# Attention followed by routed experts: routing transposed in small squares on VectorE, single units' rows made stationary, first biases computed apart

## The chip, the cores and the metric

The kernel runs on one core of one Trainium2 chip. The metric is device time in microseconds (us). The kernel before takes 783.4 us; where two kernels are compared, each was run several times on the same chip in alternation. The engines are TensorE (PE in the profile, its weight loads PEld), VectorE (DVE), ScalarE (ACT), GpSimd (POOL) and SyncE (SP).

## The reference

Selective attention over 8 batches x 8 heads x 576 positions x 64, then a mixture of 8 experts in which each token either chooses its own expert or keeps the one of the token before it:

```python
scores = scale * q @ k.T                       # causal
bias = -(cum[:, :, :, None] - cum[:, :, None, :])   # cum = cumsum(max(s, 0))
attn = softmax(where(causal, -1e9, scores + minimum(bias, 0)))
x = (attn @ v) -> (B, S, H * D)                # D of the experts = 512
for b in range(B):
    prev_e = -1
    for s in range(S):
        fresh_e = argmax(logits[b, s])         # logits = x @ w_gate, 8 experts
        e = fresh_e if s == 0 or local_gate[b, s] < 0.5 else prev_e
        prev_e = e
        h = maximum(x[b, s] @ w1[e], 0)        # 512 -> 1024
        out[b, s] = softmax(logits[b, s])[e] * (h @ w2[e])
```

## The kernel before

TensorE works through 32 pairs of heads, one after the other. Beside them the routing of finished batches runs in groups (batches 0 and 1, 2 and 3, 4, 5), its steps planned into certain pairs. The chosen expert of a token lies with tokens on the partitions; to carry it forward along the sequence ("held") it has to lie along the free axis, so it is transposed, scanned, and transposed back. Before, TensorE did both transposes, by matmuls with the identity into a bank of the score pool (banks are parts of PSUM, the memory that TensorE writes):

```python
for bs in ((0, 1), (2, 3), (4,), (5,)):
    n = HP * bs[-1] + HP + 1
    g = sort.group(bs, xs)
    at(n, 2, g.choose, g.codes)
    at(n + 1, 1, g.rows)
    at(n + 1, 2, g.fresh, g.share, g.held)
    at(n + 2, 1, g.hold)
    at(n + 2, 2, g.hot, g.gates)
    at(n + 3, 1, g.count)
    at(n + 3, 2, g.rank)
    for f in g.scatters:
        place = max(place + (2 if n < 17 else 1), 3 * (n + 4))
        at(place // 3, (3, 4, 0)[place % 3], f)
# ... (cut)
def rows(self, bank):                     # class Group
    self.codes_of = main, tails = [x[:nb] for x in bank(2)]
    for t, p, z, a in s.runs:
        # ... (cut)
        nc.tensor.transpose(y, x, i)
def fresh(self, bank):
    for x, a in zip(self.codes_of, (0, TS)):
        # ... (cut)
        nc.vector.tensor_scalar(u[:, a:z], x, 0.0, None, Alu.is_equal)
        nc.scalar.activation(v[:, a:z], x, Act.Relu, bias=self.s.minus[: self.nb])
def hold(self, bank):
    e = self.e = bank(1)[0][:, : NB * nb].rearrange("p (t b) -> p t b", b=nb)
    for t, p, z, a in s.runs:
        # ... (cut)
        nc.tensor.transpose(e[:z, t], x, i)
```

After attention come the experts in units of rows: doubles (256 rows of one expert), singles (128 rows) and mixed units (two experts of 64 rows each). The first layer of a double or a single keeps the weights stationary and moves the rows; a mixed unit keeps the rows stationary and moves the weights, 512 columns at a time, and VectorE then turns its hidden rows:

```python
def layer1(i, first, last):
    # ... (cut)
    if len(w) > 1:                        # mixed
        # ... (cut)
                for h in range(2):
                    d = slice(h * HALF, h * HALF + HALF)
                    mm(ps[d], lhsT=xT[i][:, c, d], rhs=w[h][:, c, f], start=(c == 0), stop=(c == DK - 1))
            nc.scalar.activation(hx[i][:, f], ps, Act.Relu)
        # then 16 nc.vector.transpose of hx into hT
        return
    # double or single: matmuls of n = 256 or 128 columns
                mm(y, lhsT=w[0][:, c, f : f + P], rhs=xT[i][:, c, :], start=(c == 0), stop=(c == DK - 1))
```

At the start, 18 matmuls with the identity (`spin(18)`) warm TensorE up, all biases of the exponentials are made in one block, and only then do the first scores begin.

## Time and profile before

| kernel before | value | where it is read |
|---|---|---|
| time | 783.39 us (782.95 to 784.17) | runs |
| span of the profiled execution | 782.4 us | head of the page |
| attention, first to last rows of a pair | 17.93 to 233.28, so 215.35 us | chain of waits |
| the experts' first matmul | 241.87 us | timeline |

TensorE is busy all the time, so the table to watch is where its pairs and units start. In the chain of waits the line "PE o L406 x99" comes once in each pair: the attention-weighted rows. The lines themselves stand in the prediction. Of the 576 positions the last 64 (576 = 4 x 128 + 64) are called the tail.

### The profile page before, as it was taken

The numbers are of one execution on the slowest core, as the hardware profiler recorded it, in microseconds if no ns is written. First come the engines' busy times: TensorE is split into PE (matmuls) and PEld (weight loads), VectorE is DVE, ScalarE is ACT, GpSimd is POOL, SyncE is SP. The second block draws the span as 40 slices with busy tenths as digits, with TensorE's granted clock in tenths as the row PEclk, the third lists the DMA queues.
The fourth block names the chain that finished last, engine by engine and source line by source line (L and its number), as shares of the span: only waits on it lengthen the run. The fifth ranks groups of instructions, "written<-read, shape, count | busy, mean of one in ns | idle before, by whom it ended". The sixth has DMA issues, their size and how long they took to land.

```text
span 782.4 us, 17629 instructions
## 1 busy us (share of the span) xinstructions
PE 773.0 (99%) x6782; PEld 546.2 (70%) x6782; DVE 339.0 (43%) x1196; ACT 237.2 (30%) x611; POOL 176.2 (23%) x329
## 2 busy tenths in 40 slices
PE   9999999999999999999999999999999999999996
PEld 8888888888887846836677366773657736676762
DVE  2334444455566748315562156521565215635000
ACT  5777767776762111111111111111111111111110
POOL 4432345456450421011110111101111011011001
PEclk9999999999999999999999999999999999999999
DMA  9586679988655499966997569976699766994001
GB/s 314 187 300 194 201 244 327 326 285 262 210 208 217 131 354 390 409 228 221 376 395 297 199 224 380 392 290 208 233 365 389 297 211 228 368 409 175 10 13 44
DMA packets 64141, 205.56 MB, mean 263 GB/s; under 512 B 8269, under 2 KB 8301, under 8 KB 64048
## 3 DMA queue, kind: packets, MB, share of 16 engines
q1 hardware_dynamic: 55008, 173.55, 62.3%
q0 software_dynamic: 8896, 30.47, 10.4%
q8 instruction: 55, 0.90, 0.5%
q10 hardware_dynamic: 144, 0.33, 0.1%
q14 instruction: 38, 0.31, 0.1%
HBM read 181.08 MB, written 23.76 MB: 262 GB/s over the span
## 4 chain that ended last, share of the span: by engine, by line
issue 58%; PE 32%; POOL 5%; DVE 2%; POOLq 2%; DMA 1%; DVEq 0%
PE o L406 14%; PE ps L335 11%; POOL out_dram L1261 2%; POOL xg L1196 2%; PE hp L1243 2%; PE o L374 2%; PE o L291 1%; POOLq L1171 1%; DMA x_rows<-x,r_slot_i 1%; PE o L356 1%; PE bank L956 0%; DVE xT L1097 0%; POOL x_rows L1047 0%; PE bank L1107 0%; PE bank L981 0%
## 5 line engine op out<-in xcount | busy, mean ns | idle before, releaser
L1097 DVE STREAM_TRANSPOSE xT<-xg 32x128 f32<-32x128 f32 x576 | 174.1, 302 | 174.2 <-PE hp L1243 92.7
L1256 PE MATMUL yp<-w,hT 128*128 128x512 f32 (+1 forms) x528 | 216.4, 593 | 0.0
L1243 PE MATMUL hp<-xT,w 128*128 128x256 f32 (+1 forms) x1088 | 192.3, 337 | 0.3 <-DVE xT L1097 0.3
L1243 PEld LDWEIGHTS hp<-xT,w 128*128 128x128 f32 x1088 | 172.1, 191 | 24.6 <-issue 8.2
L344 ACT ACTIVATE sc<-ps,bias 128x256 f32<-128x256 f32 (+3 forms) x448 | 156.5, 482 | 53.6 <-PE ps L335 51.2
L1256 PEld LDWEIGHTS yp<-w,hT 128*128 128x128 f32 (+1 forms) x528 | 90.1, 180 | 114.6 <-issue 113.3
L1261 POOL DMA_INDIRECT out_dram<-y,at_gate x38 | 38.5, 1013 | 433.9 <-ACT y L1260 419.0
L406 PE MATMUL o<-v,sc 128*64 128x74 f32 x3072 | 113.6, 228 | 0.8 <-issue 0.8
L406 PEld LDWEIGHTS o<-v,sc 128*64 128x64 f32 x3072 | 108.8, 136 | 8.1 <-issue 4.3
L1247 ACT ACTIVATE hT<-hp 128x512 f32<-128x512 f32 x68 | 40.6, 597 | 193.0 <-PE hp L1243 193.0
L1260 ACT ACTIVATE y<-yp,at_gate 128x512 f32<-128x512 f32 x38 | 26.1, 687 | 239.8 <-PE yp L1256 233.6
L335 PE MATMUL ps<-q,k 64*128 64x320 f32 (+2 forms) x768 | 92.5, 386 | 0.1
L350 POOL TENSOR_SCALAR_AFFINE_SELECT sc<-sc 128x256 f32<-128x256 f32 x160 | 66.5, 420 | 115.9 <-issue 59.1
L335 PEld LDWEIGHTS ps<-q,k 64*128 64x128 f32 x768 | 68.9, 186 | 20.0 <-issue 4.8
L1256 PE MATMUL yp<-x,hT 128*128 128x512 f32 (+1 forms) x144 | 63.2, 594 | 0.0
L1234 DVE STREAM_TRANSPOSE hT<-x 32x256 f32<-32x256 f32 x64 | 27.9, 436 | 65.4 <-ACT x L1228 64.5
L1243 PEld LDWEIGHTS hp<-xT,x 128*128 128x128 f32 x320 | 46.1, 191 | 5.8 <-issue 2.6
L1243 PE MATMUL hp<-xT,x 128*128 128x128 f32 (+1 forms) x320 | 50.1, 317 | 0.0
L416 DVE RECIPROCAL recs<-o 128x4 f32<-128x4 f32 x64 | 12.1, 189 | 87.0 <-PE o L406 63.1
L1256 PEld LDWEIGHTS yp<-x,hT 128*128 128x128 f32 (+1 forms) x144 | 25.3, 178 | 26.2 <-issue 26.0
L1047 POOL DMA_INDIRECT x_rows<-x,r_slot_i x40 | 38.7, 968 | 10.1 <-issue 5.9
L419 DVE TENSOR_TENSOR x<-o,recs 128x292 f32<-128x292 f32 x64 | 34.4, 538 | 2.2
(162 smaller groups left out, 339.8 us busy)
## 6 DMA issues: line engine op xcount, KB each, us to landing
w<-in_w_dram SPq DMA_DIRECT2D x184, 512.0 KB, 9.5
x<-in_w_dram SPq DMA_DIRECT2D x56, 512.0 KB, 9.3
v<-in_vx_dram SPq DMA_DIRECT2D x32, 405.0 KB, 5.8
vt<-in_vz_dram SPq DMA_DIRECT2D x32, 320.0 KB, 3.9
k<-in_kz_dram SPq DMA_DIRECT2D x31, 320.0 KB, 5.1
q<-in_q_dram SPq DMA_DIRECT2D x32, 288.0 KB, 5.4
xg<-x_rows POOLq DMA_DIRECT2D x30, 293.0 KB, 8.5
x_rows<-r_empty SPq DMA_DIRECT2D x6, 293.0 KB, 3.6
```

The lines of the kernel that those rows point to most:

```text
L335: mm(ps[:, h, at : at + z - a], lhsT=kb[d, c * P : c * P + P], rhs=qb[d, a:z], start=True, stop=True)
L344: nc.scalar.activation(scs[n, u][:, h, at : at + z - a], raw[u][:, h, at : at + z - a], Act.Exp, bias=bias[:, i : i + 1], scale=scale)
L350: nc.gpsimd.affine_select(out=x, in_=x, compare_op=Alu.is_ge, fill=0.0, base=0, pattern=[[0, 2], [1, P]], channel_multiplier=-1)
L406: mm(y, lhsT=w, rhs=x, start=start, stop=stop)
L419: nc.vector.tensor_tensor(x, y, rec.unsqueeze(3).to_broadcast([P, t1 - t0, 2, HW]), op=Alu.mult)
L1047: self.s.nc.gpsimd.indirect_dma_start(out=next(self.s.views)[:, :], out_offset=bass.IndirectOffsetOnAxis(ap=self.slot[:z, m : m + 1], axis=0),
L1097: self.nc.vector.transpose(self.xT[i][d : d + m, :, k * P + a * m : k * P + a * m + m], rows[a * m : a * m + m, :, X0[d // DH] + d % DH :] ...
L1234: nc.vector.transpose(hT[i][d : d + m, :, a : a + m], x[a : a + m, :, d : d + m])
L1243: mm(y, lhsT=w[0][:, c, f : f + P], rhs=xT[i][:, c, :], start=(c == 0), stop=(c == DK - 1))
L1247: nc.scalar.activation(hT[i][:, g : g + per], ps, Act.Relu)
L1256: mm(ps[n * m : n * m + m, :], lhsT=hT[i][:, c, a : a + m], rhs=wn[:, c, :], start=(c == 0), stop=(c == FK - 1))
L1261: nc.gpsimd.indirect_dma_start(out=next(outs)[:, :], out_offset=bass.IndirectOffsetOnAxis(ap=at[i, k][:, 0:1], axis=0), in_=y[:, :], eleme ...
```

## The change

Its intent: take the fourteen small matmuls of each routing group from TensorE and let VectorE transpose 32x32 squares instead, which needs no bank; give the single units the form that the mixed ones have, so that eight matmuls of 512 columns replace 32 of 128; and start the first scores before all biases are there. Steps of the routing after the codes move one pair later. The diff also holds small edits that are not shown: the order of work in the last pair, the last group's scatters spread over more places, and at the experts the order of one fetch and one buffer less for the results. Cut to its core:

```diff
-            at(n + 1, 1, g.rows)
-            at(n + 1, 2, g.fresh, g.share, g.held)
-            at(n + 2, 1, g.hold)
-            at(n + 2, 2, g.hot, g.gates)
-            at(n + 3, 1, g.count)
-            at(n + 3, 2, g.rank)
+            at(n + 1, 2, g.rows, g.fresh, g.share)
+            at(n + 2, 2, g.held, g.hold)
+            at(n + 3, 2, g.hot, g.gates)
+            at(n + 4, 1, g.count)
+            at(n + 4, 2, g.rank)
             for f in g.scatters:
-                place = max(place + (2 if n < 17 else 1), 3 * (n + 4))
+                place = max(place + (2 if n < 17 else 1), 3 * (n + 5))
@@ start (cut)
-    spin(18)
+    spin(8)
+    tail_scores(0)
+    scores(0, 0)
+    # biases of group 0, their copy, scores(0, 1), then biases of group 1
@@ rows
+        if self.by_squares:
+            self.erow = self.t("row", [SQ, 3, 256])
+            for p, t, i, r in self.squares():
+                nc.vector.transpose(self.erow[:, i, r], self.code_squares[p, t, :])
+            return
@@ fresh
+        if self.by_squares:
+            # ... (cut)
+            nc.vector.tensor_scalar(u, v, 0.0, None, Alu.is_equal)
+            nc.scalar.activation(v, v, Act.Relu, bias=self.s.minus[:SQ])
+            return
@@ hold
+        if self.by_squares:
+            for p, t, i, r in self.squares():
+                nc.vector.transpose(e[p, t, :], self.erow_parts[:, i, r])
+            return
@@ layer1
-        if len(w) > 1:
+        if nbs[i] == 1:
+            m = P // len(w)
-                    for h in range(2):
-                        d = slice(h * HALF, h * HALF + HALF)
-                        mm(ps[d], lhsT=xT[i][:, c, d], rhs=w[h][:, c, f], ...)
+                    for h, wh in enumerate(w):
+                        d = slice(h * m, h * m + m)
+                        mm(ps[d], lhsT=xT[i][:, c, d], rhs=wh[:, c, f], ...)
```

## The prediction

> **What bounds the kernel now.** First the page's head: which engine is full, and when.
>
> ```profile
> PE 773.0 (99%) x6782; PEld 546.2 (70%) x6782; DVE 339.0 (43%) x1196; ACT 237.2 (30%) x611; POOL 176.2 (23%) x329
> ...
> PE   9999999999999999999999999999999999999996
> PEld 8888888888887846836677366773657736676762
> DVE  2334444455566748315562156521565215635000
> ```
>
> TensorE (PE) is busy in every slice but the last, and its waits come to under 3 us (1.6 before its first instruction, 0.8 and 0.3 where attention meets the experts). VectorE (DVE) has more than half of its time free. So a microsecond is gained where PE is given less to do, or where its weight loads wait, and work moved to DVE is free until it delays something that PE needs. Next the chain of waits, cut to the attention, where PE's pairs of heads follow each other (start, length, what):
>
> ```profile
> 72.30 3.42 PE o L406 x99
> ...
> 79.09 3.42 PE o L406 x99
> ...
> 87.04 3.42 PE o L406 x99
> ...
> 94.63 3.42 PE o L406 x99
> ...
> 102.43 3.42 PE o L406 x99
> ...
> 109.23 3.42 PE o L406 x99
> ```
>
> The distance of two starts is the cost of a pair: 6.79 plain, then 7.95, 7.59 and 7.80 us, then 6.80. These three long pairs are the routing of one group: codes turned to rows, experts turned back ("hold"), ranks counted. The timeline of the same stretch says why:
>
> ```profile
> 83.50 0.34 DVE L377 STREAM_TRANSPOSE v<-o 128x160 f32<-128x160 f32 x1
> ...
> 84.16 2.88 PE L335 MATMUL ps<-q,k 64*128 64x320 f32 x24
> 84.26 0.81 DVE L965 TENSOR_SCALAR r_u<-bank 2x512 f32<-2x512 f32 x2 [0.41 <-PE bank L956]
> 84.97 0.88 ACT L966 ACTIVATE r_v<-bank,r_minus 2x512 f32<-2x512 f32 x2 [2.10 <-DVE r_u L965]
> ...
> 85.76 0.91 ACT L344 ACTIVATE sc<-ps,bias 128x320 f32<-128x320 f32 x2
> ...
> 101.30 0.84 PEld L335 LDWEIGHTS ps<-q,k 64*128 64x128 f32 x8 [0.54 <-DVE r_rank L1015]
> ```
>
> In the first two long pairs PE only does extra matmuls. In the third its scores also wait 0.54 us for a bank of PSUM that DVE's ranking still reads. Last the experts (timeline of PE): one single unit, its first layer and its second.
>
> ```profile
> 364.69 7.31 PE L1243 MATMUL hp<-xT,w 128*128 128x128 f32 x64
> 371.93 7.09 PE L1256 MATMUL yp<-w,hT 128*64 128x512 f32 x32
> 378.94 7.41 PE L1243 MATMUL hp<-xT,x 128*128 128x128 f32 x64
> 386.19 7.03 PE L1256 MATMUL yp<-w,hT 128*128 128x512 f32 x16
> 393.06 13.98 PE L1243 MATMUL hp<-xT,w 128*128 128x256 f32 x64
> ```
>
> From start to start, layer 1 of a single takes 7.25 us (378.94 to 386.19) and its layer 2, as many multiplications in wide matmuls, 6.87 us (386.19 to 393.06). The records are two for each matmul: 113 ns for one of 128 columns, 429 ns for one of 512, so 4 x 107.
>
> **What the Trainium skill says.** "TensorE: Matmul & The Clock Gate", Back-to-back issue gap, gives a warm gap of columns/2.4 plus about 2.5 ns. If a float32 record is two passes, that is 429 ns at 512 and 109 at 128; the trace has 429 and 113, so the narrow matmul pays a little more, and its 191 ns weight load sits before each. The same page, What you observe and What's actually happening, says that the array runs at half clock until about 3.4 us of busy time are past, and falls back when idle. The trace agrees in kind: the warm-up matmuls at the start go at 6 or 7 records per us up to 7.0 us and at 12 after it, though the granted clock reads 1.00 throughout. The same page, Architectural detail, says that ScalarE and VectorE are strictly first in, first out; in the lines above ScalarE's exponentials (L344) start only when the code rows' relu (L966), which waited for DVE, is done. "VectorE: DVE Perf Modes", The three transpose paths, says that VectorE turns 32x32 blocks only; the trace has 302 ns for four such blocks, 436 for eight, hence an estimate of 235 ns for two, 268 for three.
>
> **The change part by part.**
>
> *Routing by squares, four groups.* Seven matmuls for the codes and seven for the experts go from PE in each group. Over the four groups the excess of the pairs over 6.79 us is 1.155 + 1.155 + 1.15 + 1.15 = 4.6 us for the codes, 4 x 0.795 = 3.2 for the experts, and 1.0 + 1.0 + 0.85 + 0.85 = 3.7 for the counting, 11.5 in all (which is also what the whole attention has over 30 plain pairs: 215.35 less 30 x 6.795). The first two go: 7.8 us. The counting stays, but it now comes one pair later, and so no longer after the 1.07 us of DVE work on the logits that come every fourth pair; the 0.54 us wait for the bank should go, and some 0.4 in the other two groups. I take 1.7 of the 3.7 as saved, leaving 0.5 each for its own matmuls. That makes 9.5 us.
>
> Against it: DVE gets 8 transposes for the codes, 2 x 0.28 + 6 x 0.25 = 2.05 us with the spacing that the trace shows (315 for a 302), and as many a pair later. DVE has 2.25 us of work in a plain pair (19.1 in 57.6 us), so it can take that. But the relu of the code rows sits in ScalarE's order ahead of the next pair's exponentials, and now waits for the 8 transposes. Counted in the trace of before without the code matmuls: the next scores would start at 82.92, DVE is free at 83.84, squares until 85.9, the comparison (some 0.5) until 86.4, relu until 87.05. Exponentials normally start 1.24 us after the scores, at 84.16 here: 2.9 us late. They take 5.0 us, so they end at 92.05, and PE wants the last of the three score banks at 82.92 + 6.79 + 1.86 = 91.57. PE waits some 0.55 us with the semaphore, once in each group: minus 2.2 us. Net of this part: 7.3 us.
>
> *Singles with rows stationary, ten units.* 32 matmuls of 128 columns (7.25 us) become 8 of 512 (16 records at 429 ns, 6.87 us): 0.38 us each, 3.8 us. ScalarE writes the same two pieces per unit. DVE gets 16 transposes of eight blocks, 7.20 us each time (L1234, as the mixed units have them now), 72 us in all. The closest spot is mixed, single, single, double. Layer 1 of the first single ends at t = 0; ScalarE is done at 0.8, DVE turns the hidden rows until 8.1, then the double's two inputs, 2 x 5.25, until 18.6. PE meanwhile has the mixed layer 2 (7.0), the next single's layer 1 (6.9) and this single's layer 2 (6.9): it wants the double's inputs at 20.8. Slack 2.2 us, and the hidden rows are wanted at 13.9, ready at 8.1. At the end (double before the last single) 13.8 us lie between. I count no loss.
>
> *First group's biases apart.* Before, the exponentials start at 10.86 after 18 warm-up matmuls and all biases. Now PE stops at about 4.1 after 8, then waits for q, which lands at about 7.2 by the order of the loads. If the array were warm: scores until 8.3, first bias at 8.9, 1.5 us gained by the first pair. But PE idles for 3 us, so scores run at half clock (an estimate from the first 5 us of the trace): scores to 9.6, transposes 10.05, bias ready at 10.6, the second bias at 12.1, and the first pair ends about where it did. I put 0.2 us down.
>
> *The rest.* The first layer 2 goes ahead of the fetch for the third unit, so that fetch comes after one more write on GpSimd, 1.7 us later (284.2 for 282.5). Its inputs were turned by 298.8 and wanted at 302.2; there is still slack. The scatters spread over more hooks keep their order on GpSimd. The last pair's order changes nothing, as PE waits there (0.83 us) for DVE's transposed gates. Zero.
>
> Sum: 7.3 + 3.8 + 0.2 = 11.3 us, so 783.4 - 11.3 = 772.1 us, a gain of 1.4%.
>
> **Rivals.** (1) ScalarE's order costs nothing, because the banks come free earlier than I count or DVE's squares are shorter: then 9.5 + 3.8 + 0.2 = 13.5, 770 us; with a warm start besides, 768.5. For it: ScalarE has 1.8 us free in each pair; against it: the strict order above. (2) DVE becomes the bound among the experts: the slack of 2.2 us is used up by late fetches (turning waited for a fetch nine times, 62 us in all), PE waits some 2 us at each of five runs of singles and the gain of the singles is gone: 776 us. For it: DVE's queue is in order, and a turn that waits for its fetch holds up the hidden rows behind it; against it: in the trace the double's rows landed 11.3 us after the single's layer 1 started, well before DVE would want them. (3) The cold start costs instead of saving, up to 1.5 us: 774. (4) The early rows are fetched after scatters that now come a pair later; were they late, DVE would stand still before the last pairs. I count 3 us of slack, so this is unlikely.
>
> **Range and chances.** The rivals span 768.5 to 776, and that is my range. Faster by over 2% needs 767.7, more than every term at its best gives (9.5 + 3.8 + 1.5 = 14.8, 768.6): 0.06. Slower by 2% needs a new stall of 27 us: 0.01.
>
> **What would show it.** Layer 1 of a single at 6.87 us from start to start and no PE wait on DVE's hT; long pairs at 7.3 (one pair after the codes), 6.79 (experts) and 7.3 (counting); PE waiting on ScalarE's exponentials once in each group, about half a microsecond; DVE busy for about 339 + 72 + 16 = 427 us; first exponentials between 9 and 10.7 us. I am wrong if PE waits for hT or xT among the experts for more than 2 us in all, or if the attention's pairs keep their old length.

## The result, and the profile after

The changed kernel takes 773.0 us (median of four runs, 771.58 to 776.38) against 783.5 us (782.95 to 784.17) for the kernel before on the same chip. The ratio is 0.9872, with a 95% interval of 0.9838 to 0.9906: within 2%. Ratios here are the mean time of one kernel's fast runs over the mean of the other's of the same rounds, so they are not quite the ratio of the medians quoted. The mean granted clock of the profiled executions is 0.995 to 0.999, except for e11 (0.988).

The profiled execution of the changed kernel, span 774.7 us, is the slowest of its four. That matters below. From the head of its page:

```profile
PE 762.5 (98%) x6198; PEld 499.3 (64%) x6198; DVE 417.2 (54%) x1417; ACT 236.8 (31%) x608; POOL 175.8 (23%) x333
...
PE   8999999999999999999999999999999999999996
...
DVE  2233643666676839415992159921599215977130
```

TensorE has 584 fewer matmul records and 10.5 us less busy time, and is still busy in every slice but the last; the first slice went from 9 to 8. VectorE went from 339.0 to 417.2 us (427 predicted), with slices at 9 among the experts.

Where did the 7.7 us between the two profiled spans come from? Cut at the same places:

| stretch | before, us | after, us | difference |
|---|---|---|---|
| until the first rows in the chain | 17.93 | 20.93 | +3.00 |
| attention, first to last rows | 215.35 | 207.42 | -7.93 |
| last rows to experts' first matmul | 8.59 | 8.59 | 0 |
| experts to the end | 540.5 | 537.8 | -2.8 (rounded) |

**Attention.** The chain of waits of the changed kernel, over the stretch whose counterpart of before is in the prediction:

```profile
82.10 3.42 PE o L422 x99
88.89 3.42 PE o L422 x99
95.69 3.42 PE o L422 x99
102.48 3.42 PE o L422 x99
109.88 3.42 PE o L422 x99
```

The pairs take 6.79, 6.80, 6.79 and 7.40 us. The pairs with the codes and with the experts are plain; only the counting is left, 0.60 us of its own matmuls (four such pairs: 7.40, 7.40, 7.36, 7.36). The prediction had one pair of 7.3 after the codes. The timeline says why it is not there:

```profile
81.71 0.31 ACT L378 ACTIVATE tail<-o,bias 128x64 f32<-128x64 f32 x1
...
86.03 2.86 PE L307 MATMUL ps<-q,k 64*128 64x320 f32 x24
...
86.77 1.51 DVE L986 STREAM_TRANSPOSE r_row<-r_code 32x96 f32<-32x96 f32 x8
...
88.79 0.78 ACT L1005 ACTIVATE r_row<-r_row,r_minus 32x576 f32<-32x576 f32 x1 [2.92 <-DVE r_u L1004]
...
89.47 0.91 ACT L365 ACTIVATE sc<-ps,bias 128x320 f32<-128x320 f32 x2
...
90.30 0.29 ACT L378 ACTIVATE tail<-o,bias 128x64 f32<-128x64 f32 x1
...
95.06 0.29 ACT L378 ACTIVATE tail<-o,bias 128x64 f32<-128x64 f32 x1
```

The relu (L1005) does hold ScalarE back: it waited 2.92 us for VectorE, and the exponentials start at 89.47, which is 3.44 us after their scores (86.03). But the eight transposes took only 1.51 us, and the delay is gone one pair later. The tail's exponential (L378) shows that: it starts 2.48 us after the pair's scores in a plain pair (81.71, scores at 79.23), 4.27 us after them in the delayed pair (90.30 from 86.03), and 2.23 us after them in the next (95.06 from 92.83). ScalarE catches up by working without gaps, and TensorE doesn't wait.

One pair is longer than planned, 8.00 us. In it TensorE waits for VectorE, and VectorE for a transfer:

```profile
134.48 0.46 DVE L435 TENSOR_TENSOR x<-o,recs 128x292 f32<-128x292 f32 x1 [1.78 <-DMA x_rows<-x,r_slot_i]
...
135.00 0.48 PE L390 MATMUL o<-vt,wz 128*32 128x160 f32 x8 [1.13 <-DVE x L435]
```

There are four buffers for the rows of a batch. The fifth batch writes over those of the first, whose scatters to memory now start one pair later and have not all been read out. That costs 1.21 us once, and no part of the prediction named it. (e9 has the same wait for 0.6 us on another chip.)

**The start.** Timelines of the first 18 us. Before:

```profile
10.86 0.95 ACT L344 ACTIVATE sc<-ps,bias 128x320 f32<-128x320 f32 x2 [7.98 <-PE ps L335]
...
12.41 2.05 PE L291 MATMUL o<-ident 128*128 128x128 f32 x16
```

After:

```profile
6.52 0.48 PE L313 MATMUL o<-q,k 128*64 128x64 f32 x4 [1.19 <-DMA q<-in_q_dram]
6.93 2.08 PE L307 MATMUL ps<-q,k 64*128 64x320 f32 x8
...
9.82 0.95 ACT L365 ACTIVATE sc<-ps,bias 128x320 f32<-128x320 f32 x2 [1.65 <-DVE bias L349]
...
14.49 2.98 PE L292 MATMUL o<-ident 128*128 128x128 f32 x16
```

The first exponentials come 1.0 us earlier. But TensorE ran slow for longer: the same 16 records of the second warm-up take 2.98 us instead of 2.05, and end 3.0 us later (17.47 against 14.46). The trace's own clock records agree: the full clock is first noted at 16.47 us here and at 7.41 us before (read from the packed trace; the views print 1.00 for the stretch that has no record). This loss is one of this execution, as the experiments show.

**Singles.** Timeline of TensorE, then of VectorE:

```profile
373.74 7.13 PE L1282 MATMUL hp<-x,xT 128*128 128x512 f32 x16
380.71 7.03 PE L1312 MATMUL yp<-w,hT 128*128 128x512 f32 x16
387.58 13.98 PE L1299 MATMUL hp<-xT,w 128*128 128x256 f32 x64
```

```profile
367.46 7.18 DVE L1290 STREAM_TRANSPOSE hT<-x 32x256 f32<-32x256 f32 x16 [8.19 <-ACT x L1284]
...
379.86 5.04 DVE L1150 STREAM_TRANSPOSE xT<-xg 32x128 f32<-32x128 f32 x16
```

Layer 1 of a single takes 6.97 us from start to start (373.74 to 380.71), not 7.25 as before and not the 6.87 predicted; the two singles at the very end take 6.87, where they took 7.14 before. No wait for `hT` is among TensorE's waits, and its only one for `xT` is the 0.3 us of before. The second line shows VectorE done with the double's inputs at 384.9 (a little later with two small copies), 2.5 us before TensorE wants them at 387.58.

### The profile page after: what moved, and what is told of

Read it like the earlier page. It is cut to its first block, busy times and chain, and to the rows that moved or that the text cites.

```text
span 774.7 us, 16687 instructions
## 1 busy us (share of the span) xinstructions
PE 762.5 (98%) x6198; PEld 499.3 (64%) x6198; DVE 417.2 (54%) x1417; ACT 236.8 (31%) x608; POOL 175.8 (23%) x333
## 3 DMA queue, kind: packets, MB, share of 16 engines
q0 software_dynamic: 8896, 30.47, 10.5%
## 4 chain that ended last, share of the span: by engine, by line
issue 56%; PE 30%; DMA 4%; POOL 4%; DVE 3%; POOLq 1%; SPq 1%; DVEq 0%
PE o L422 13%; PE ps L307 12%; POOL out_dram L1317 2%; DMA x<-in_w_dram 2%; POOL xg L1249 2%; PE hp L1299 2%; PE o L390 2%; DMA w<-in_w_dram 1%; POOLq L1224 1%; DMA x_rows<-x,r_slot_i 1%; PE o L313 1%; DMA q<-in_q_dram 1%; SPq L1112 1%; DVE xT L1150 1%; PE o L292 0%
## 5 line engine op out<-in xcount | busy, mean ns | idle before, releaser
L1290 DVE STREAM_TRANSPOSE hT<-x 32x256 f32<-32x256 f32 x224 | 97.6, 436 | 133.1 <-ACT x L1284 130.1
L1299 PE MATMUL hp<-xT,w 128*128 128x256 f32 x640 | 140.9, 380 | 0.3 <-DVE xT L1150 0.3
L1299 PEld LDWEIGHTS hp<-xT,w 128*128 128x128 f32 x640 | 121.1, 190 | 20.6 <-issue 4.2
L307 PE MATMUL ps<-q,k 64*128 64x320 f32 (+2 forms) x768 | 95.0, 393 | 0.6 <-DVE bias L349 0.6
L307 PEld LDWEIGHTS ps<-q,k 64*128 64x128 f32 x768 | 71.3, 191 | 20.7 <-issue 6.3
L1282 PE MATMUL hp<-w,xT 128*128 128x512 f32 (+1 forms) x208 | 77.7, 595 | 0.0
L1303 ACT ACTIVATE hT<-hp 128x512 f32<-128x512 f32 x48 | 28.6, 597 | 134.4 <-PE hp L1299 134.4
L1282 PEld LDWEIGHTS hp<-w,xT 128*128 128x128 f32 (+1 forms) x208 | 29.7, 165 | 46.5 <-issue 46.5
L1284 ACT ACTIVATE x<-hp 128x512 f32<-128x512 f32 x28 | 16.7, 597 | 79.1 <-PE hp L1282 79.1
```

Of the source, the lines that this page charges most:

```text
L307: mm(ps[:, h, at : at + z - a], lhsT=kb[d, c * P : c * P + P], rhs=qb[d, a:z], start=True, stop=True)
L1282: mm(ps[d], lhsT=xT[i][:, c, d], rhs=wh[:, c, f], start=(c == 0), stop=(c == DK - 1))
L1290: nc.vector.transpose(hT[i][d : d + m, :, a : a + m], x[a : a + m, :, d : d + m])
L1303: nc.scalar.activation(hT[i][:, g : g + per], ps, Act.Relu)
```

## The experiments

Eleven kernels ran, in three sittings on three other chips. All three were slower for every kernel: the kernel before takes 796.6 to 797.5 us there, with granted clocks like the above. So each run is compared with the runs of before in its own sitting. The whole change ran again there as a control (e5): 782.72 us, ratio 0.9813. So on these chips the same change gains 14 us (13.8 by the medians, 14.9 by the ratio) instead of 10.5; that difference is taken up at the end of this section.

The parts first.

**e1_old_start: the whole change with the old start put back.**

```diff
-    spin(8)
+    spin(18)
-    tail_scores(0); scores(0, 0)   # first scores ahead of the biases
+    # all biases in one block, then tail_scores(0), scores(0, 0) in the loop
```

> The changed kernel with the start of the kernel before put back (18 warm-up matmuls, all biases ahead of the first scores). Theory A (the new start is cold and costs time, up to 3 us, differently in each execution): first attention rows at 17.9 us as in the kernel before instead of 20.9, time 770 to 771 us, and all executions within 1 us of each other. Rival B (the start is not the cause of the spread of 771.6 to 776.4; it is the fetches or DVE among the experts): the spread stays and the median stays near 773.

Measured: 781.34 us (779.08 to 781.93), ratio 0.9808 (0.9788 to 0.9828). The control with the new start has 0.9813 (0.9791 to 0.9835), in another sitting. The start makes no difference that can be measured, which here means to within some 2 us. The executions spread over 2.9 us, not within 1 us as theory A had it, so the start is not the only source of the spread.

**e2_new_start_only: the kernel before with the new start alone**, the same edit the other way round.

> The kernel before with nothing but the new start. Theory A: 783.5 plus 0 to 3 us, with executions several us apart. Rival (the new start gains by itself and only loses beside the rest): 782 or less. In both, the pairs of the attention from the second on keep their old distances.

Measured: 797.58 us, ratio 1.0008 (0.9988 to 1.0028), or +0.6 us with an interval from -1.0 to +2.2. So the 3.0 us that the first pair of profiles suggests is not what the new start typically costs; up to 2.2 us is not excluded.

**e3_singles_only: the kernel before with the singles' edit alone.**

```diff
-        if len(w) > 1:
+        if nbs[i] == 1:
```

(with `m` and `hx` as in the change)

> The kernel before with the singles' rows stationary and nothing else. Theory: ten units save 0.28 us each, as the trace of the changed kernel shows start to start (6.97 for 7.25), so 780.7 us, and no wait of TensorE on hT. The prediction on record would have had 0.38 each, 779.7. Rival (DVE becomes a bound): 783 or more.

Measured: 794.05 us, ratio 0.9976 (0.9958 to 0.9993), so 1.9 us (0.6 to 3.3) gained. In its trace layer 1 of a single takes 6.96 or 6.97 us in every run of singles, as in the changed kernel. The trace gives 10 x 0.28 = 2.8 us, inside that interval; the predicted 3.8 is outside.

**e4_squares_twice: the whole change with the codes' squares issued twice**, result unchanged.

```diff
-            for p, t, i, r in self.squares():
-                nc.vector.transpose(self.erow[:, i, r], self.code_squares[p, t, :])
+            for _ in range(2):
+                for p, t, i, r in self.squares():
+                    nc.vector.transpose(self.erow[:, i, r], self.code_squares[p, t, :])
```

> The changed kernel with each of the four groups' eight code transposes issued twice (the same result). It tests the mechanism that the prediction priced at 2.2 us and that the trace shows as 0: ScalarE's exponentials wait for the relu, which waits for the transposes. In the trace the exponentials end 0.6 us before TensorE wants the bank. If the mechanism is real, 1.5 us more of transposes makes TensorE wait about 0.9 us in each group, 3.6 us in all, seen as pairs of 7.7 us in place of 6.8. If ScalarE's order does not matter, the pairs stay at 6.8 and the time does not move.

Measured: 789.59 us (785.8 to 793.16), ratio 0.9926 (0.9888 to 0.9964), 8.2 us worse than e1 of the same sitting, which differs from it by the start and the doubled squares; its four executions lie in two groups, 785.8 and 786.67, 792.52 and 793.16, the slower two at a lower granted clock (0.992 and 0.997, for 0.999). The pairs after the codes are now 8.24, 8.25, 9.47 and 9.50 us. From TensorE's waits, and from the timeline of the third group:

```profile
PE o L422 <- ACT tail L378: 7.4, 4, 2.5
```

```profile
171.02 3.19 DVE L987 STREAM_TRANSPOSE r_row<-r_code 32x96 f32<-32x96 f32 x16
...
176.57 1.44 PE L422 MATMUL o<-v,sc 128*64 128x74 f32 x35 [2.45 <-ACT tail L378]
```

(The columns of the first fence are: total wait in us, times, longest.) So the mechanism of the prediction is real: ScalarE's order can hold TensorE up, and by more than I expected here (pairs of 7.7, 3.6 us in all). But what TensorE waits for is not one of the three score banks, as I had put it, but the exponential of the tail (L378), which reads the bank that the pair's second half of rows is written to. With 1.5 us of squares there is a little room, with 3.2 us there is none. In the changed kernel of the first chip the tail's exponential ends at 90.59 (90.30 + 0.29) and the matmul that waits in e4, the 89th record of the pair, starts at 90.93; so some 0.3 us are left. (In e4's first two groups 1.68 us more of squares brought a wait of 1.22, which makes it 0.46.)

**e5_after_again: the changed kernel itself, as control.**

> The changed kernel as it is, so that it stands on one chip beside its variants (the chip of the last runs gave 796.8 us for the kernel before, where the first gave 783.5). If the gain is the same kind of work everywhere: 0.987 of the kernel before. If the old start is worth 2 us or more, as the first trace says, it is behind the variant with the old start by that much, and its executions spread more.

Measured: 782.72 us (779.25 to 783.6), ratio 0.9813 (0.9791 to 0.9835). Its start lasts 2.1 us less than in the first profile (the scores of the third pair begin at 22.80 instead of 24.87). The pair of 8.00 us isn't there; the pairs of that stretch take 7.13 and 6.93. TensorE waits 0.9 us for the tail's exponential in two pairs, those after the codes of the third and fourth groups. The squares take 1.51 us there too, but they begin 1.94 and 1.38 us after the pair's scores, for 0.74 in the first profile, so the room above is not enough on every chip.

**e6_scatter_early: the first group's scatters one to each third of a pair until place 45**, meant to free the first buffer sooner.

```diff
-                place = max(place + (2 if n < 17 else 1), 3 * (n + 5))
+                place = max(place + (2 if n < 17 and place > 45 else 1), 3 * (n + 5))
```

> The changed kernel with the first batch's five scatters one place after another (places 42 to 46 for 42 to 50), so that they have landed before VectorE writes the fifth batch over the same buffer. Theory: the pair of 8.0 us in which TensorE waited 1.1 us for the gates and VectorE 1.8 us for the scatter becomes a plain one of 6.8; 1.2 us less than the changed kernel. Rival: the earlier scatters delay the masks on GpSimd or the weights that load in the same pairs, and nothing is gained.

Measured: 781.77 us, ratio 0.9821 (0.9806 to 0.9837): no gain over the control. The wait that it was to remove was not in the control either; and pairs of 7.51 and 7.89 us, for 6.94 and 7.07 in the control, appeared where the scatters now lie closer (in e7 and e8 too). That is the rival of the expectation. That the 1.21 us of the first profile can be had back in this way is not shown.

**e7_best_old_start: early scatters and the old start together.**

> Both at once: the old start and the early scatters. Theory: the old start's worth (0 to 4.8 us by execution, 2 to 3 on average) and 1.2 us; about 3.5 us below the changed kernel, 769.5 where the kernel before takes 783.5, and a spread of 1 us.

Measured: 782.12 us, ratio 0.9818 (0.9804 to 0.9832). No better than the change.

**e8_best_spin14: early scatters, and the new start with 14 warm-up matmuls instead of 8**, so that TensorE is not idle before `q` lands.

```diff
-    spin(8)
+    spin(14)
```

> The early scatters and the new start, but with 14 warm-up matmuls for 8, so that TensorE is busy until about 6.3 us, close to when q lands. If the cold array is what the new start costs, then the scores run at full rate, the first exponentials start at about 9 us and the second pair's rows at about 16.5, one us ahead of the old start: 768.5 where the kernel before takes 783.5. If what it costs is the order (second bias behind the scores of the second unit), it stays behind the old start.

Measured: 782.4 us, ratio 0.9825 (0.9811 to 0.9838). No better either. Its scores of the third pair begin at 20.95 us, among the early ones.

What these say of the start together: the scores of the third pair begin, by the traces, at 21.86, 20.65, 20.65, 21.92 and 21.50 us in the five executions profiled with the old start (before, e1, e3, e7, e9), and at 24.87, 22.80, 22.50, 20.79, 20.51, 20.39 and 22.84 with the new one (after, e5, e2, e4, e6, e10, e11). The new start is sometimes the best and sometimes 4 us behind; on average it is 0.8 us later. The difference is whether the array runs fast, here in e6, whose trace first notes the full clock at 5.91 us:

```profile
6.72 1.14 PE L307 MATMUL ps<-q,k 64*128 64x320 f32 x8
...
11.05 2.05 PE L292 MATMUL o<-ident 128*128 128x128 f32 x16
```

The same eight records took 2.08 us in the first profile of the change, and the sixteen 2.98. The Trainium skill, "TensorE: Matmul & The Clock Gate", What's actually happening, says that the busy window behind the array's clock is free-running, so that the number of slow matmuls at the start differs from run to run. These traces agree, with a spread of 4.5 us here.

**e9_squares_only: the whole change with the start and the singles put back.**

```diff
+    spin(18)              # and all biases in one block, as in e1
-        if nbs[i] == 1:
+        if len(w) > 1:
```

> The change with its start and its singles put back: only Routing's codes and experts turned in squares are left of it. If the parts add up, as theory says, this keeps the attention's gain (8 to 10 us on a chip like the first, up to 12 on the slower one), lacks only the singles' 2 to 3 us, and so comes out some 2 to 3 us above the whole change sent beside it. If the attention's gain needed the new start or the rest, it keeps less than 6.

Measured: 786.99 us (785.2 to 787.25) against 797.45 for before, ratio 0.9861 (0.9842 to 0.9879), so 11.1 us (9.6 to 12.6) by the ratio. The routing, with the small edits at the experts that this run keeps, carries most of the gain. e10, which is the whole change but for one instruction, is 3.5 us better in the same sitting. The ratios of the parts (routing 11.1, singles 1.9, start -0.6) sum to 12.4 us, and the whole gave 14.9 (e5). With an interval of some 1.5 us on each, the remainder of 2.5 us can't be called an interaction.

**e10_relu_on_vector: the whole change, with the code rows' relu on VectorE**, so that nothing in ScalarE's order waits for the squares.

```diff
-            nc.scalar.activation(v, v, Act.Relu, bias=self.s.minus[:SQ])
+            nc.vector.tensor_scalar(v, v, -1.0, 0.0, Alu.add, Alu.max)
```

> The whole change, but the code rows' relu runs on VectorE instead of ScalarE, so ScalarE's order holds nothing that waits for the squares. Theory: the change itself stands half a microsecond short of a stall at this place, so nothing is gained on a chip like the first, and up to 2 us where the trace shows TensorE waiting for the tail's exponential; its waits on the tail in the pairs after the codes are gone. Rival (my prediction's ScalarE stall is there but hidden in the trace): 2 us gained everywhere.

Measured: 783.45 us (782.51 to 785.21), ratio 0.983 (0.9811 to 0.9849). TensorE's wait for the tail's exponential is gone from the trace (e9 and e11, whose relu is on ScalarE, have 2.3 us of it in the same sitting), but the time is not better than the control's ratio of 0.9813. The test is not clean, though. VectorE's order is now 0.45 us longer, and in the fourth group TensorE waits for VectorE instead:

```profile
203.35 0.48 PE L390 MATMUL o<-vt,wz 128*32 128x160 f32 x8 [1.25 <-DVE x L435]
```

From the third pair's scores to the experts' first matmul e10 takes 217.8 us and e11, which has the change's routing, 218.0. So 2.3 us of waits went and 0.2 us was gained. The rival, 2 us gained everywhere, is not what happened; what ScalarE's stall alone is worth on these chips is not shown.

**e11_hidden_twice: the whole change with the singles' hidden rows turned twice**, result unchanged.

```diff
-                for a in range(0, P, m):
-                    for d in range(0, P, m):
-                        nc.vector.transpose(...)
+                for _ in range(2 if len(w) == 1 else 1):
+                    for a in range(0, P, m):
+                        for d in range(0, P, m):
+                            nc.vector.transpose(...)
```

> The whole change with the singles' hidden rows turned twice by VectorE, some 7 us more of VectorE work in each single unit, results unchanged. Theory: a single's layer 2 waits for all its hidden rows, and VectorE has 2.5 us of slack before the double that follows two singles; so TensorE should wait some 4 to 5 us more in each run of two singles and a double, about 20 us in all, with waits named hT or xT. Rival (VectorE's time among the experts is really free, as its busy share says): under 3 us.

Measured: 829.63 us (827.02 to 833.36), ratio 1.0413; 46 us worse than e10 of the same sitting. VectorE's busy time is 69.5 us above that of the first profile of the change (486.7 for 417.2), so 7.0 for each of the ten singles. Timelines of TensorE and of VectorE in the first run:

```profile
391.28 7.13 PE L1313 MATMUL yp<-w,hT 128*128 128x512 f32 x16 [1.57 <-DVE hT L1291]
401.59 10.60 PE L1300 MATMUL hp<-xT,w 128*128 128x256 f32 x48 [3.17 <-issue]
```

```profile
376.29 14.93 DVE L1291 STREAM_TRANSPOSE hT<-x 32x256 f32<-32x256 f32 x32 [8.20 <-ACT x L1284]
...
396.45 5.04 DVE L1150 STREAM_TRANSPOSE xT<-xg 32x128 f32<-32x128 f32 x16
```

TensorE's layer 2 starts when the hidden rows are turned (376.29 + 14.93 = 391.22), and the double when its inputs are: VectorE's transposes end at 401.49, and TensorE goes on at 401.59, although the profile calls that wait "issue". My expectation counted one single to a run; there are two, each with its own extra turn. TensorE's next five phases, from start to start, are longer than e5's by 1.7, 3.4, 1.2, 3.4 and 1.8 us, 11.6 in all; the four such runs lose 11.6, 9.9, 11.6 and 6.4 us, 39.5 together. The theory stands, and the rival (under 3 us) falls; my expectation of 20 us had the wrong count. The first two phases, up to the double, are what it was about: 5.2 us, for 4 to 5 expected.

Not all of the loss is waiting. The fifth phase has no wait. In it TensorE's clock is lower (columns: stretch, us, TensorE busy and records, granted clock, DMA share, GB/s):

```profile
427.00:431.00 4.00, 4.00 (x11) 0.57 0.92 294
```

Records that stood 0.216 us apart stand 0.427 apart there. In three of the four runs the trace notes half the clock with or just after a wait of 3.2 us, for 3.4, 6.8 and 3.4 us, which is some 6.6 of the 39.5 us. A stall can thus cost TensorE more than its own length.

The slack that the prediction worked out, 2.2 us, is about right (2.5 read from the trace of the change; here the hidden rows take 14.93 us for 7.18, 7.75 more, and the double starts 5.2 later, so 2.6), so VectorE, at 54% by its share, stands some 2.5 us from being the bound there.

**What stays open.** Why the three later chips are slower, and why the change gains 14 us there. The traces say where. Among the experts both kernels lose alike: from the first expert matmul to the end e5 takes 542.5 us (537.8 on the first chip) and e3, whose singles are the change's, 542.8. TensorE waits 2.5 to 2.9 us there between about 270 and 290 us in every later profile but e8 (1.1), and in six of the eleven the granted clock then halves for 3.4 us (0.57 from 274 to 278 us in e5); the first chip's profiles have neither. The extra gain lies in the attention: from the third pair's scores to the first expert matmul the change saves 7.9 us on the first chip (220.0 to 212.1), and in one later sitting e1 takes 215.7 and e3, with the old routing, 228.5. In these traces TensorE's pairs are a few tenths of a microsecond longer from about 105 us on: e5's five pairs from 105 to 140 us take 6.93 to 7.13 us, and four of e3 there, which have no group's steps in them, 6.96 to 7.12, for 6.80 on the first chip. From 150 us on e3's pairs take up to 8.7 us, e5's up to 7.8. The waits named in e3 are seven of 2.8 us in all with "issue" as their cause, which says nothing. e3's first expert matmul comes at 249.17 (241.87 for before on the first chip, 7.3 later although its start was 1.2 us shorter), e5's at 238.49 (236.94 on the first chip). So kernels with the old routing lose more to whatever it is. No run separates its cause, and the landings of the transfers are missing from those traces.

## Why the prediction was right or wrong

It was right in the total, 772.1 against 773.0 us, and within 2% as the likeliest outcome. It was right by terms that make up for one another, so the closeness of the total is in part luck.

- *The small matmuls of codes and experts leave TensorE, 7.8 us, and 1.7 of the counting's 3.7.* Right in mechanism and nearly in size. What remains above plain pairs in the profile after is some 4 x 0.59 = 2.36 us of counting (2.0 predicted); 11.5 less 2.36 is 9.1 of the 9.5 us predicted.
- *ScalarE's order takes 2.2 us back.* Wrong, in two steps. The eight transposes were priced at 2.05 us and took 1.51 (205 ns each for 64 columns and 245 for 96, and they overlap), and the exponentials at 5.0 us, where ScalarE, without gaps, takes some 4.7 (from 89.47 to the next pair's first, about 94.2). And the dependency that binds is not the third score bank but the tail's exponential (e4). Rival (1), that this order costs nothing, is what the first chip showed; on others 0.9 to 2.3 us of such waits are in the trace, near the 2.2 in size, but in the third and fourth groups only and not once in each. Whether they cost as much in time is not shown (e10).
- *A wait that was not foreseen*: 1.21 us, once, for the first batch's scatters, which the change moves a pair later. The prediction looked at the scatters for the experts' fetches only, not for the buffers that they read. It is in the first chip's profile and, with 0.6 us, in e9; the control on another chip does not have it. Net of this part: 7.9 us, 7.3 predicted.
- *Singles, 0.38 us each.* Mis-sized: 0.28, 2.8 us in all (e3 and both profiles). The working compared 7.25 of a layer 1 with 6.87 of a layer 2. But that layer 1 borders on a mixed unit's layer (64 rows stationary), and the layer 2 taken as a measure does not. The border has 0.1 us of its own, before and after the change: next to a mixed layer a single's layer 1 took 7.24 to 7.25 and takes 6.96 to 6.97; at the very end, away from one, it took 7.14 and takes 6.87.
- *The start, 0.2 us.* Right as a median (e1, e2: no difference to be seen), wrong as an account of one execution: in the profile it costs 3.0 us, in others it saves 1. Rival (3) had the mechanism, with 1.5 us at most. The prediction's reading of the warm-up was off: it has 6 or 7 records per us and 12 after. The view by stretches gives such counts, since it counts a record on an edge in both stretches. Their starts are 0.21 us apart up to 7.26 us and 0.11 apart after it, a factor of two.
- *Rival (2), VectorE as the bound.* It did not come about; e11 shows how near it is.
- *The sum for a float32 record.* It counts the 2.5 ns once for two passes; counted twice it gives 432 and 112 ns, an estimate too, where the trace has 429 and 113. So it does not show that the narrow matmul pays more. The singles at the end do: 7.14 us in 64 records for 6.87 in 16 four times as wide.

With the start at its median of 0 the terms sum to 7.9 + 2.8 = 10.7 us, and the runs gave 10.5.

## What to carry to other kernels

When an engine is full, moving its small helper work to one with time left is worth about what that work costs in the trace, but ask for each moved step what it stands in front of in a queue that keeps its order, and what buffer its later readers hold. An engine at half load can be 2.5 us from setting the time: count its slack between two things that the full engine wants, not by its share. And before you trust a few microseconds at the start of one profile, look at several executions.

## What the Trainium skill lacked or had wrong

- "VectorE: DVE Perf Modes", The three transpose paths, gives one duration, 311 ns for 128x128 in bf16. The runs show for float32 on 32 partitions 205 to 208 ns for 64 columns, 245 to 267 for 96, 302 for 128 and 436 for 256; eight in a row of the two smallest took 1.51 us. So 64 columns cost some two thirds of 128, and the page's one figure does not carry over to narrow squares.
- "TensorE: Matmul & The Clock Gate", What's actually happening, says that the number of slow matmuls at the start varies, puts the penalty under 1% of a typical span and advises not to fit to a count. The runs agree: the start of the third pair's scores moved between 20.39 and 24.87 us with the same start, 4.5 us of some 775. What no page says is that the granted clock printed by the profile reads 1.00 in the slow stretch too, because the trace's clock records begin only with the full clock (at 16.47 us in the first profile of the change, 5.91 in e6).
- No page has the 0.1 us that a layer costs where it borders on one with 64 rows stationary: eight float32 matmuls of 512 columns took 6.96 to 6.97 us there and 6.87 elsewhere.
- No page says that the profile can name "issue" as the end of a wait that another engine's work seems to have ended: in e11 TensorE stood for 3.17 us until 401.59, and VectorE's transposes of its inputs ended at 401.49.
